# The end of an attention and feed-forward kernel: block transposes on VectorE, halves in the last tile, and another rule table

## The chip, the cores and the metric

The kernel runs on one core of one Trainium2 chip. The time is the device time of one execution in microseconds. Five engines work side by side: TensorE (PE, matmuls and the weight loads that go with them), VectorE (DVE), ScalarE (ACT), GpSimd (POOL) and SyncE (SP, which issues nearly all DMAs). Each engine runs its own instructions in the order in which they were written down; semaphores order the engines against each other.

## The reference

One transformer block with modulated layernorms, on 2048 tokens of width 512, in bfloat16. What matters of it:

```python
mod = (_silu(c) @ w_mod).reshape(c.shape[0], 6, 1, -1)       # sa, ca, ga, sb, cb, gb
h = _layernorm(x) * (1 + ca) + sa
qkv = h @ wqkv                                               # 32 heads of 16
p = softmax(q @ k.T * 16 ** -0.5);  o = p @ v                # all 2048 keys for every query
x = x + ga * (o @ wo)
h = _layernorm(x) * (1 + cb) + sb
x = x + gb * ((gelu(h @ w_gate) * (h @ w_up)) @ w_down)      # inner width 1792
```

The costly part is the softmax: 32 x 2048 x 2048 exponentials, cut below into 2048 blocks of 128 x 512.

## The kernel before, in words

**Units, rounds, blocks.** The queries are cut into seven sets (`SETS`): two of 512, three of 256, two of 128 queries. A unit is one set and one "quad" of four heads (`qd`, 0 to 7); the four heads lie on four groups of 32 partitions. For `qd` 0 and 1 the last two sets form one unit. A unit walks over the keys in rounds of four blocks, a block being 128 x 512 scores. The whole stream has 2048 blocks, and `pos` is the number of the next one.

A block goes through three steps. PE makes the scores (`qk`, into one of six banks of `ps_sc`). Then the exponential: either ACT takes two or three blocks in one instruction (`E<-ps_sc`), or DVE takes a block by a bit trick (`bits`, a TENSOR_SCALAR from `ps_sc` to uint16) and finishes four of them together with two masks and a product on 128 x 2048 (`power_task`). Last, PE multiplies with the values and with a column of ones (`pv_mms`), so that the accumulator `ps_pv` holds for each head 16 output rows and one row, number `DH` = 16, with the softmax's denominator.

**Who sets the order.** The program is planned while it is built. `stream` keeps a predicted time for each engine (`model`) and picks PE's next work step by step: scores for ACT, scores for DVE, attention matmuls, or side work (projections, output projection, feed-forward of finished sets, in windows that `plan` sets). `task` holds DVE, ACT and SP steps that wait for their operands; `urgency` orders them. The choices are governed by `RULES`, one row for every 64 positions, 32 rows in all, with the fields

```python
_Rule = collections.namedtuple("_Rule", "ready hole back fill lag early alone ahead side2")
```

`fill` is the column floor: `short(t)` is `fill` minus the columns that PE has streamed in the last 3413 ns of predicted time (a matmul on a quarter of the array counts a quarter). When it is above zero and ACT has enough work ahead, PE gets a filler matmul whose result nobody reads (`ps_mi<-xs,ident` and the like). `early` and `alone` bound when a block is given to DVE (beside ACT's blocks, or alone), `back` and `ahead` how many quads of blocks DVE may have open and how far ahead, `lag` when side work goes first.

**The end of a unit.** `unit_end` copies the accumulator to `osb`. For most units the denominators then go to DRAM and back (`scr_den`, `den`), are inverted as 128 x m numbers, go out again and come back spread over the 16 rows of each head (`rb`), and DVE multiplies. The last units have no time for that: for `PEN` (quads 6 and 7 of set 5, quads 5, 6 and 7 of set 6) `near_end` spreads the denominator with an fp32 matmul with a selection matrix (`self32`) on PE, DVE takes the reciprocal of the whole 128 x 128 result and multiplies into `onorm`. `near_end` runs as side work in the window of set 5, between the pieces of `side_last`, and for the very last quad first of all in `tail_end`.

**The tail.** After the last attention matmul two generators share PE: `tail_end` for set 6 (the last tile of 128 tokens) and `tail_rest` for what is left of the feed-forward of set 5. `tail_end` makes the output projection of its tile in one bank (a residual matmul, then one product per quad), the layernorm (`ln_stat`, `ln2_steps`, the norm into `E`), two pairs of transposes on PE, each pair into one bank, four modulations (ACT and DVE in turn), and `tail_ffn`: gate matmuls, gelu on ACT, up matmuls, product on DVE, down projection of 512 columns in one bank, `down_fin` (times `gb`, plus the residual, one DMA out). `tail_rest` has gate and up results of set 5 stored (`gate5`, `up5`); in four pieces it takes the gelu (`g5`), the product (`p5`) and the down projection. Products 0 and 1 wait for the last quad's `onorm`, products 2 and 3 for the last norm (`ln2`); the next product is posted when the piece before has been issued.

The recorder (`rec`) makes two engines that read the same bank of PSUM wait for each other.

## Time and profile before

| | us |
|---|---|
| median of 3 runs (lowest, highest) | 821.74 (820.31, 822.78) |
| the profiled execution, its own time | 824.7 |
| its span, first to last instruction | 823.0 |
| ACT busy | 793.5 (96%) |
| DVE busy | 756.9 (92%) |
| PE busy (pipelined, so not at its peak) | 752.0 (91%) |
| first exponential, last exponential's end | 16.4, 801.13 |
| mean granted TensorE clock | 0.99 |

The span is the stretch between the first and the last instruction of the profiled execution; all times of the trace count from its start. A row of the timeline has start, length, engine, line of the kernel, operation, and output <- inputs with their shapes; a bracket behind it is the idle time ahead and what ended it. A row by form has instead the number of instructions, their busy time in us and the mean of one in ns. Lines 375, 394, 398, 406 and 415 are helpers (`mm`, `act`, `tt`, `ts`, `copy`) through which most instructions go, so rows are told apart by the names of their tiles.

### The profile page before, as it was taken

The numbers are of one execution on the slowest core, as the hardware profiler recorded it, in microseconds if no ns is written. First come the engines' busy times: TensorE is split into PE (matmuls) and PEld (weight loads), VectorE is DVE, ScalarE is ACT, GpSimd is POOL, SyncE is SP. The second block draws the span as 40 slices with busy tenths as digits, with TensorE's granted clock in tenths as the row PEclk, the third lists the DMA queues.
The fourth block names the chain that finished last, engine by engine and source line by source line (L and its number), as shares of the span: only waits on it lengthen the run. The fifth ranks groups of instructions, "written<-read, shape, count | busy, mean of one in ns | idle before, by whom it ended". The sixth has DMA issues, their size and how long they took to land.

```text
span 823.0 us, 30418 instructions
## 1 busy us (share of the span) xinstructions
PE 752.0 (91%) x13786; PEld 302.8 (37%) x13788; DVE 756.9 (92%) x1366; ACT 793.5 (96%) x743; POOL 4.6 (1%) x13
## 2 busy tenths in 40 slices
PE   8899999988898998899988989999999898999997
PEld 3333333322222222222233333333543354356574
DVE  7757999999999999999999999999999999799775
ACT  5989999999999999999999999999999999999992
POOL 2000000000000000000000000000000000000000
PEclk9979999999999999999999999999999999999999
DMA  8101000000001311110003212110653242330000
GB/s 283 51 2 29 16 11 9 3 10 9 9 10 35 107 49 35 41 47 21 17 17 97 62 48 57 45 35 12 175 162 98 69 128 87 85 101 11 18 10 14
DMA packets 77212, 43.73 MB, mean 53 GB/s; under 512 B 21269, under 2 KB 75482, under 8 KB 77082
## 3 DMA queue, kind: packets, MB, share of 16 engines
q1 hardware_dynamic: 77080, 41.78, 18.0%
q8 instruction: 108, 1.77, 0.9%
q14 instruction: 22, 0.18, 0.1%
q10 hardware_dynamic: 2, 0.00, 0.0%
HBM read 39.15 MB, written 2.60 MB: 51 GB/s over the span
## 4 chain that ended last, share of the span: by engine, by line
ACT 75%; PE 19%; DVE 5%; issue 0%; DMA 0%; DVEq 0%
ACT E L394 73%; PE ps_sc L375 9%; PE ps_mi L375 7%; PE ps_pv L375 3%; ACT hreg L394 2%; DVE mreg L406 1%; ACT L394 1%; DVE dreg L406 1%; PE ps_mi L379 0%; DMA xs<-in_A_x_dram 0%; DVE st L434 0%; DVE hreg L415 0%; DVE mreg L398 0%; DVE wo L422 0%; DVE wreg L398 0%
## 5 line engine op out<-in xcount | busy, mean ns | idle before, releaser
L394 ACT ACTIVATE E<-ps_sc 128x1024 bf16<-128x1024 f32 (+1 forms) x702 | 747.2, 1291 | 8.8 <-PE ps_sc L375 8.3
L375 PE MATMUL ps_sc<-qT,kmo 32*128 32x256 bf16 (+2 forms) x1728 | 199.8, 295 | 27.2 <-ACT E L394 23.6
L375 PE MATMUL ps_sc<-qT,kme 32*128 32x256 bf16 (+2 forms) x1728 | 193.1, 295 | 22.0 <-ACT E L394 18.6
L406 DVE TENSOR_SCALAR mreg<-ps_sc 128x512 uint16<-128x512 f32 x256 | 171.4, 685 | 12.6 <-PE ps_sc L375 10.5
L375 PE MATMUL ps_pv<-E,vaug 128*17 128x256 bf16 (+2 forms) x2720 | 148.6, 291 | 0.9 <-DVE osb L415 0.6
L375 PE MATMUL ps_mi<-wreg,mreg 128*32 128x256 bf16 (+2 forms) x1872 | 107.5, 327 | 2.6 <-DVE hreg L415 1.2
L375 PEld LDWEIGHTS ps_sc<-qT,kme 32*128 32x128 bf16 x1728 | 56.5, 92 | 144.5 <-ACT E L394 123.5
L406 DVE TENSOR_SCALAR dreg<-ps_sc 128x512 uint16<-128x512 f32 x156 | 104.0, 684 | 4.8 <-PE ps_sc L375 3.3
L375 PEld LDWEIGHTS ps_sc<-qT,kmo 32*128 32x128 bf16 x1728 | 58.3, 92 | 132.8 <-ACT E L394 112.4
L375 PEld LDWEIGHTS ps_pv<-E,vaug 128*17 128x17 bf16 x2720 | 53.6, 89 | 55.1 <-issue 40.1
L406 DVE TENSOR_SCALAR mreg<-mreg 128x2048 uint16<-128x2048 uint16 x100 | 67.8, 683 | 0.2
L375 PEld LDWEIGHTS ps_mi<-wreg,mreg 128*32 128x32 bf16 (+1 forms) x1872 | 41.9, 96 | 42.3 <-issue 18.8
L375 PE MATMUL ps_pv<-mreg,vaug 128*17 128x256 bf16 (+2 forms) x856 | 50.7, 298 | 2.4 <-DVE mreg L398 1.7
L398 DVE TENSOR_TENSOR mreg<-mreg 128x2048 bf16<-128x2048 bf16 x36 | 43.6, 1216 | 0.1
L398 DVE TENSOR_TENSOR mreg<-dreg,mreg 128x2048 bf16<-128x2048 bf16 x34 | 41.1, 1209 | 0.0
L375 PE MATMUL ps_mi<-hreg,wreg 128*32 128x512 bf16 x480 | 40.3, 393 | 0.8 <-DVE qT L406 0.5
L415 DVE CAST hreg<-ps_mi 128x512 bf16<-128x512 f32 x49 | 33.6, 686 | 2.1 <-PE ps_mi L375 1.6
L398 DVE TENSOR_TENSOR dreg<-mreg,dreg 128x2048 bf16<-128x2048 bf16 x27 | 32.7, 1213 | 0.0
L375 PE MATMUL ps_mi<-wo,onorm 128*32 128x512 bf16 x416 | 31.0, 383 | 1.1 <-DVE wreg L398 0.5
L398 DVE TENSOR_TENSOR hreg<-ps_mi,hreg 128x512 bf16<-128x512 f32 x46 | 31.5, 685 | 0.3 <-PE ps_mi L375 0.2
L406 DVE TENSOR_SCALAR dreg<-dreg 128x2048 uint16<-128x2048 uint16 x44 | 29.9, 680 | 0.0
L375 PE MATMUL ps_mi<-mreg,hreg 128*32 128x512 bf16 x352 | 28.8, 384 | 0.0
(174 smaller groups left out, 689.7 us busy)
## 6 DMA issues: line engine op xcount, KB each, us to landing
mreg<-in_B_w_up_dram SPq DMA_DIRECT2D x32, 256.0 KB, 2.9
mreg<-in_B_w_gate_dram SPq DMA_DIRECT2D x28, 256.0 KB, 3.5
mreg<-in_B_w_down_dram SPq DMA_DIRECT2D x16, 256.0 KB, 2.7
dreg<-in_B_w_down_dram SPq DMA_DIRECT2D x12, 256.0 KB, 4.8
mreg<-in_w_mod_dram SPq DMA_DIRECT2D x1, 2048.0 KB, 12.0
rb<-scr_rec SPq DMA_DIRECT2D x64, 32.0 KB, 1.8
out_dram<-xs SPq DMA_DIRECT2D x16, 128.0 KB, 1.8
rb<-scr_rec SPq DMA_DIRECT2D x104, 16.0 KB, 1.7
```

The lines of the kernel that those rows point to most:

```text
L375: return self.rec("pe", lambda e: e.matmul(out, lhsT, rhs, start=start, stop=stop, tile_position=tp), [lhsT, rhs, *after], [out], cost=(n, ...
L394: return self.rec("act", lambda e: e.activation(out, in_, func, scale=scale, **kw), rd, wr, cost=self.cost("act", out, [in_], "act") + load)
L398: return self.rec(eng, lambda e: e.tensor_tensor(out, a, b, op), [a, b], [out], cost=self.cost(eng, out, [a, b], "tt"))
L406: return self.rec(eng, lambda e: e.tensor_scalar(out, a, s1, s2, **kw), rd, [out], cost=self.cost(eng, out, [a], "ts") + (60 if len(rd) > ...
L415: return self.rec(eng, lambda e: e.tensor_copy(out, in_), [in_], [out], cost=self.cost(eng, out, [in_], "ts"))
```

## The change

1. **Normalisation of the `PEN` quads.** `near_end` and its places in the side work are gone. `unit_end` transposes the accumulator in blocks of 32 x 32 on DVE, from PSUM into `osb`; a query is then a partition, and its denominator one column. DVE inverts 128 x 4 numbers, multiplies with them broadcast, into bf16, and transposes the blocks back into `onorm`. The three later steps are one task of the urgent class.
2. **The last tile.** The norm is written as two halves of 256 columns. Each of the four transposes has a bank of its own (5, 3, 2, 1). The down projection accumulates two halves of 256 columns in two banks (`ps_mi` and bank 2), and each half has its own product, addition and DMA, 64 KB each.
3. **Products of set 5.** Products 0 to 2 wait for the last `onorm`, product 3 for the norm; all four are posted ahead of the down projection.
4. **The rule table.** 23 of the 32 rows have other values. Row 0's floor goes from 2700 to 4200, row 28's from 2000 to 3900; three others (rows 12, 18 and 20) go down to 3600; the lowest floor in the table is 3300.
5. `TAILPV`, `TIE` and `GRP` are new names that have, at the values given, the effect of what stood there before.

```diff
-    (30, 50, 8, 2700, 1536, 400, 3200, 20, 1800),
-    (80, 100, 8, 4200, 1536, 400, 3200, 20, 2500),
+    (80, 300, 8, 4200, 1536, 400, 1600, 20, 1800),
+    (80, 50, 8, 4200, 1536, 400, 1600, 20, 3200),
...
-    (60, 200, 8, 3900, 2048, 500, 1900, 20, 2500),
-    (60, 50, 8, 3300, 768, 500, 1900, 12, 2500),
-    (80, 200, 8, 3300, 1536, 850, 3200, 12, 3200),
-    (30, 300, 8, 3300, 1536, 850, 1900, 28, 3200),
-    (30, 300, 8, 3300, 1536, 850, 1900, 28, 3200),
-    (30, 200, 8, 3300, 768, 850, 3200, 16, 3200),
-    (15, 200, 8, 3900, 2048, 500, 1900, 24, 2500),
-    (30, 200, 9, 3600, 2048, 500, 2500, 24, 2500),
-    (30, 200, 8, 4200, 2048, 500, 3200, 24, 2500),
-    (30, 200, 8, 4200, 1536, 500, 3200, 24, 2500),
+    (30, 200, 8, 3600, 2048, 500, 1300, 20, 1800),
+    (60, 50, 8, 3300, 768, 500, 1900, 12, 3200),
+    (80, 200, 8, 3300, 1536, 850, 3200, 12, 1024),
+    (30, 300, 8, 3300, 1536, 850, 4000, 28, 3200),
+    (30, 300, 8, 3300, 1536, 850, 4000, 28, 3200),
+    (5, 200, 8, 3300, 768, 850, 1600, 16, 3200),
+    (15, 200, 8, 3600, 2048, 500, 1900, 24, 2500),
+    (30, 200, 9, 3600, 2048, 500, 2500, 24, 1800),
+    (15, 200, 8, 3600, 2048, 500, 1600, 24, 3200),
+    (30, 200, 8, 4200, 1536, 500, 4000, 24, 2500),
...
-    (80, 200, 10, 3600, 2048, 650, 2500, 24, 1800),
+    (5, 50, 7, 4200, 2560, 850, 1900, 20, 700),
...
-    (80, 300, 8, 2000, 1536, 500, 2500, 16, 2500),
-    (80, 100, 10, 3900, 1536, 300, 2500, 32, 2500),
-    (45, 200, 8, 3300, 1024, 300, 2500, 24, 1024),
-    (80, 100, 10, 3900, 1536, 300, 2500, 32, 1800),
+    (80, 300, 6, 3900, 3500, 500, 2500, 16, 2500),
+    (80, 50, 10, 4200, 2048, 650, 1900, 20, 1800),
+    (80, 50, 10, 4200, 3500, 0, 1900, 20, 1800),
+    (80, 50, 11, 4200, 3500, 1100, 1900, 20, 1800),
...
+    def blocks32(self, out, in_):
+        return self.rec("dve", lambda e: e.transpose(out, in_), [in_], [out], cost=self.cost("dve", out, [in_], "bn"))
...
+        if src is not None:
+            dst = self.normed(k, 0)
+            return steps + [lambda h=h: self.ln_norm(a, dst[:, h], src[:, h]) for h in (slice(0, 256), slice(256, D))]
...
+    def down_half(self, bank, t, h, i, x):
+        if x == 0:
+            self.tt("dve", self.xw[:, h], bank, self.gb[:, h], ALU.mult)
+            return
+        self.tt("dve", self.xs[:, t, h], self.xs[:, t, h], self.xw[:, h], ALU.add)
+        self.dma("sp", self.out[0, P * t:P * t + P, h], self.xs[:, t, h], "out%d" % ((t + i) % 4))
...
+        if len(sets) == 1 and qd in PEN.get(sets[0], ()):
+            self.blocks32(osb, acc[:, 0:W])
+            k = sets[0]
+            part = osb.rearrange("p (b r) -> p b r", r=32)
+            norm = rb.bitcast(BF16)[:, 0:W]
+            rec = self.rden[:, b, o:o + m]
+
+            def back():
+                self.blocks32(self.onorm[:, qd, OCOL[k]:OCOL[k] + W], norm)
+                if self.probing is None:
+                    self.live.pop(u)
+            self.task([lambda: self.recip(rec, part[:, :, DH]),
+                       lambda: self.tt("dve", norm.rearrange("p (b r) -> p b r", r=32), part,
+                                       rec.rearrange("p (b o) -> p b o", o=1).broadcast_to([P, m, 32]), ALU.mult),
+                       back], ("onorm", k, qd))
+            return
...
+PART5 = (0, 4, 8, 12, NFC)
+WHEN5 = (("onorm",), ("onorm",), ("onorm",), ("ln2",))
...
-        early, late = self.after([("onorm", last, 7)]), self.after([("ln2", last)])
-        when = (early, early, late, late)
+        when = [self.after([WHEN5[j] + (last, 7)[:1 + (WHEN5[j] == ("onorm",))], ("g5", j)]) for j in range(len(part))]
...
-        for h in range(2):
-            pb = self.scp[:, 4 + h, :]
-            yield lambda h=h, pb=pb: self.transp(pb, lambda t: self.normed(k, t), 1, h)
-            for i in range(2):
-                dc = 2 * h + i
-                self.modulate("act" if i == 0 else "dve", self.t2T[:, dc, c0:c0 + W],
-                              pb.bitcast(BF16)[:, W * i:W * i + W], self.modB, dc)
-        yield from self.tail_ffn(k, self.mi[:, :], (0, 1, 2, 3, 4, 5), 4)
+        for dc in range(NDC):
+            pt = self.scp[:, (5, 3, 2, 1)[dc], :].bitcast(BF16)[:, 0:W]
+            yield lambda dc=dc, pt=pt: self.transpose(pt, self.normed(k, 0)[:, P * dc:P * dc + P], self.ident[:, :])
+            self.modulate("act" if dc % 2 == 0 else "dve", self.t2T[:, dc, c0:c0 + W], pt, self.modB, dc)
+        yield from self.tail_ffn(k, (self.mi[:, 0:256], self.scp[:, 2, 0:256]), (0, 1, 2, 3, 4, 5), 4)
```

## The prediction

> **What bounds the kernel now.** I read the chain of waits first, then cut the span at the first exponential (16.4 us), at the two ends of the one stretch where ScalarE (ACT) is visibly idle, and at the last exponential (801.13 us).

> ```profile
> ACT 75%; PE 19%; DVE 5%; issue 0%; DMA 0%; DVEq 0%
> ...
> 16.40:37.90 21.50, 16.71 (x239) 5.88 (x239) 17.89 (x58) 21.50 (x20) 0.00 (x0) 1.00 0.33 123
> 37.90:52.60 14.70, 14.37 (x151) 5.56 (x150) 7.49 (x19) 10.38 (x10) 0.00 (x0) 0.54 0.00 1
> 52.60:801.13 748.53, 690.76 (x13051) 273.63 (x13054) 708.44 (x1224) 746.92 (x689) 0.31 (x1) 1.00 0.18 49
> 801.13:823.00 21.87, 16.36 (x217) 10.76 (x203) 11.62 (x28) 6.73 (x13) 0.00 (x0) 1.00 0.04 14
> ```

> In the windows the engines stand in the order PE, weight loads, VectorE (DVE), ACT, POOL, then the granted clock. From 52.60 to 801.13 ACT is idle for 748.53 - 746.92 = 1.6 us: nothing but less ACT work, that is exponentials moved to DVE, can shorten that stage. Two places are different. Between 37.90 and 52.60 ACT stands still for 14.70 - 10.38 = 4.32 us while the granted clock is 0.54. After 801.13 comes a tail of 21.87 us in which no engine is full and a serial chain decides.

> **The clock drop.** The half clock holds for 51.58 - 37.93 = 13.65 us, four times 3.41 us, so I laid windows of 3.41 us on its edges.

> ```profile
> 31.10:34.52 3.42, 2.51 (x30) 0.67 (x28) 3.25 (x12) 3.42 (x4) 0.00 (x0) 1.00 0.02 5
> 34.52:37.93 3.41, 2.26 (x24) 0.64 (x25) 3.30 (x17) 3.41 (x4) 0.00 (x0) 1.00 0.00 0
> 37.93:41.34 3.41, 3.41 (x25) 1.61 (x24) 2.48 (x9) 3.14 (x3) 0.00 (x0) 0.50 0.00 0
> ...
> 51.58:55.00 3.42, 3.19 (x38) 1.21 (x39) 2.72 (x6) 2.93 (x4) 0.00 (x0) 1.00 0.01 2
> ```

> The window just ahead of the drop has TensorE (PE) at 2.26 of 3.41 us. Its matmuls by form, and the exponentials that ACT had done since 16.4 us:

> ```profile
> L375 PE MATMUL ps_pv<-E,vaug 128*17 128x512 bf16 x8 | 0.8, 385 | 0.0
> L375 PE MATMUL ps_sc<-qT,kmo 32*128 32x512 bf16 x5 | 0.8, 384 | 1.2 <-ACT E L394 1.2
> L379 PE MATMUL ps_mi<-ident,dreg 128*128 128x128 bf16 x4 | 0.6, 238 | 0.0
> L375 PE MATMUL ps_sc<-qT,kme 32*128 32x512 bf16 x3 | 0.4, 385 | 0.1
> L375 PE MATMUL ps_mi<-xs,ident 128*32 128x512 bf16 x4 | 0.4, 379 | 0.0
> ...
> L394 ACT ACTIVATE E<-ps_sc 128x1536 bf16<-128x1536 f32 x10 | 15.8, 1578 | 0.0
> L394 ACT ACTIVATE E<-ps_sc 128x1024 bf16<-128x1024 f32 x10 | 11.4, 1138 | 0.0
> ```

> A matmul on 32 rows or 17 or 32 columns fills a quarter of the array, so the planner counts a quarter of its columns: (8 + 5 + 3 + 4) x 512 / 4 + 4 x 128 = 3072 columns. The planner's own log works in the same 3413 ns (`short`), and the rule in force sets how many columns it keeps in them. ACT had done 10 x 3 + 10 x 2 = 50 blocks of 512 columns, so the position is below 64 and row 0 of the table rules: its floor is 2700, the second lowest of the 32. 3072 satisfies it, and no filler is due. The change sets 4200 there. Going from 3072 to 4200 takes 1128 / 512 = 2.2 more fillers (the x4 row is one: four quarter matmuls at once, 0.4 us), 0.9 us, and PE has 3.41 - 2.26 = 1.15 us idle in the window. The filler goes out only while the planner sees slack on ACT, so I cost it at nothing; without that cover it would be at most the 0.9 us a window.

> [...]

> The gain is bounded by 0 (the drop stays) and 4.32 us (all ACT idle there). Part of the idle time is k projections that the next key group needs; DVE, at 3.30 of 3.41 us with their layernorm, paces those at any clock. I take **3.9 us**.

> **The tail.** What follows the last attention matmul, from the timeline, and one row by form:

> ```profile
> 802.03 0.29 DVE L415 COPY osb<-ps_pv 128x128 f32<-128x128 f32 x1 [0.28 <-PE ps_pv L375]
> ...
> 802.38 0.49 PE L375 MATMUL ps_sc<-osb,self 128*128 128x128 f32 x2 [0.40 <-DVE osb L415]
> ...
> 802.90 0.96 DVE L418 RECIPROCAL rb<-ps_sc 128x128 f32<-128x128 f32 x1 [0.38 <-PE ps_sc L375]
> 802.92 1.46 PE L375 MATMUL ps_sc<-wo,onorm 128*128 128x512 bf16 x6
> 803.89 0.29 DVE L398 TENSOR_TENSOR onorm<-osb,rb 128x128 bf16<-128x128 f32 x1
> 804.10 0.42 DVE L398 TENSOR_TENSOR hreg<-hreg 128x512 bf16<-128x512 bf16 x1
> ...
> 804.43 0.38 PE L375 MATMUL ps_sc<-wo,onorm 128*128 128x512 bf16 x1
> ...
> 804.85 0.70 DVE L434 BATCH_NORM_STATS2 st<-ps_sc 128x6 f32<-128x512 f32 x1 [0.32 <-PE ps_sc L375]
> ...
> 805.68 0.39 DVE L398 TENSOR_TENSOR hreg<-hreg 128x512 bf16<-128x512 bf16 x1
> ...
> 807.26 0.81 DVE L406 TENSOR_SCALAR E<-ps_sc,mv,rstd 128x512 bf16<-128x512 f32 x1
> ...
> 808.12 0.40 PE L379 MATMUL ps_sc<-ident,E 128*128 128x128 bf16 x4 [0.96 <-DVE E L406]
> 808.45 0.81 ACT L394 ACTIVATE wreg<-ps_sc,modB 128x128 bf16<-128x128 bf16 x2 [2.21 <-PE ps_sc L379]
> ...
> 809.01 0.69 DVE L406 TENSOR_SCALAR wreg<-ps_sc,modB 128x128 bf16<-128x128 bf16 x2 [0.61 <-ACT wreg L394]
> ...
> L418 DVE RECIPROCAL rden<-den 128x4 f32<-128x4 f32 x3 | 0.5, 167 | 0.0
> ```

> *Normalisation.* Before: copy, fp32 sum on PE, a reciprocal of 128x128, a product; 802.03 to 803.89 + 0.29 = 804.18, 2.15 us. After, on DVE alone: block transpose, reciprocal of 128x4 (0.17), product (0.29), block transpose back, with some 0.03 between dependent steps. No row shows a DVE transpose. From below the copy of the same 128x128 shape, 0.29; from above the slowest row on that shape, the reciprocal, 0.96. It moves data as the copy does, so I take 0.29: 0.29 + 0.17 + 0.29 + 0.29 + 0.1 = 1.14, done at 803.17. With 0.96 each it would be 2.48, done at 804.51.

> [...]

> *The wait that follows.* PE's output projection no longer stands behind the sum. The residual matmul and seven of the eight products start right behind the attention matmuls, about 801.85 (an estimate: their result reaches the copy at 802.03 some 0.2 us after issue) instead of 802.92, at 0.216 apart (six span 1.46, the last lasting 0.38: 1.08 / 5). Eight of them hold PE until 803.58, later than 803.17: PE is now what is late, and the last product goes out at 803.6 instead of 804.43. The statistics start 0.83 us earlier. (With transposes of 0.96 they would start 0.1 us later than now.) The steps from statistics to norm (2.41 us) are the same; one product of the other tile stands in them (805.68, 0.39) and still may, as its later wait is only dropped for the third piece.

> *Norm in halves.* 512 columns take 0.81. At 1.07 ns a column, from the copy (128 columns, 0.29) to the statistics (512, 0.70), a half takes about 0.54, and the next instruction starts some 0.08 before one ends (the product at 803.89 lasts 0.29, the one behind it starts at 804.10). Counted from the norm's start: first half done 0.54, second 1.0 (0.81 before, later). The transposes, each in a bank of its own, give ACT its first piece at 0.92, 0.27 earlier than the 808.45 - 807.26 = 1.19 of now. More counts that DVE no longer waits for ACT's reading of a shared bank (the 0.61 of idle before 809.01). ACT 0.92 and 1.38, DVE 0.99 and 1.44, all done at 1.83; now 809.01 + 0.69 - 807.26 = 2.44. That is 0.61 us. Bounds: 0 if the extra instruction eats it, 0.8 if DVE is quite free.

> *Down projection in halves.*

> ```profile
> 818.94 0.59 PE L375 MATMUL ps_mi<-hreg 128*128 128x512 bf16 x2
> 819.58 0.69 DVE L398 TENSOR_TENSOR wreg<-ps_mi,gb 128x512 bf16<-128x512 f32 x1 [0.87 <-PE ps_mi L375]
> 820.30 0.42 DVE L398 TENSOR_TENSOR xs<-xs,wreg 128x512 bf16<-128x512 bf16 x1
> 820.75 0.36 SPq L444 DMA_DIRECT2D out_dram<-xs  x1
> ```

> 28 matmuls of 256 columns stream what 14 of 512 did. The first half's product (about 0.42) runs while the second half finishes, but four DVE instructions replace two, and SP issues two DMAs, 0.36 us each, the second behind the first. I take 0.1 us, bounds -0.3 and +0.4. Tail: 0.83 + 0.61 + 0.1 = **1.5 us**, between 0.3 and 2.0.

> **The middle.** Five quads lose 0.29 + 0.96 + 0.29 of DVE for 0.29 + 0.17 + 0.29 + 0.29: 5 x 0.50 = 2.5 us of DVE freed, and five sums of PE (0.49 each). What DVE time buys:

> ```profile
> L406 DVE TENSOR_SCALAR mreg<-ps_sc 128x512 uint16<-128x512 f32 x256 | 171.4, 685 | 12.6 <-PE ps_sc L375 10.5
> L406 DVE TENSOR_SCALAR dreg<-ps_sc 128x512 uint16<-128x512 f32 x156 | 104.0, 684 | 4.8 <-PE ps_sc L375 3.3
> L406 DVE TENSOR_SCALAR mreg<-mreg 128x2048 uint16<-128x2048 uint16 x100 | 67.8, 683 | 0.2
> L398 DVE TENSOR_TENSOR mreg<-mreg 128x2048 bf16<-128x2048 bf16 x36 | 43.6, 1216 | 0.1
> ...
> L394 ACT ACTIVATE E<-ps_sc 128x1024 bf16<-128x1024 f32 x441 | 431.6, 1156 | 1.5 <-PE ps_sc L375 1.4
> L394 ACT ACTIVATE E<-ps_sc 128x1536 bf16<-128x1536 f32 x227 | 329.3, 1568 | 0.4 <-PE ps_sc L375 0.2
> ```

> A quad (four blocks) on DVE takes 4 x 0.685 + 2 x 0.683 + 1.216 = 5.3 us and frees 4 x (1.568 - 1.156) = 1.65 us of ACT. 2.5 us buy 0.47 quads, **0.8 us**. The other rules decide how many quads there are: 412 blocks, 103 quads now. DVE's idle 748.53 - 708.44 = 40 us would hold 7.5 more (12 us); a table that gives DVE fewer costs 1.65 each without a floor in the trace. Rows go both ways (the `alone` bound, above which DVE takes blocks by itself, falls in nine rows and rises in rows 15, 16 and 21), so I take 0 and allow two quads, 3.3 us, either way.

> **Sum.** 3.9 + 1.5 + 0.8 = 6.2 us. The profiled execution took 824.7 us; it would take 818.5. It stands 3.0 above the median of 821.74, so against the median I forecast **815.5 us**.

> **Rivals.**
> 1. The clock drop stays. For it: the floor is kept in the planner's predicted time, and PE has room only where ACT's lead lets fillers out. Against: with floors of mostly 3300 and more the middle ran at a mean of 1.00 (the 52.60 row). Price 3.9: 819.4.
> 2. Slower: the table gives DVE fewer quads. Place: ACT from 52.60 to 801.13, full already, so each lost quad is 1.65 us on the end. For it: `early` falls from 300 to 0 in row 30, `alone` doubles in rows 15 and 16. Against: the end has idle DVE and row 31 goes the other way. It decides from 824.2 on, 8.7 / 1.65 = 5.3 quads, fewer than 391 blocks on DVE; with six lost, 825.4.
> 3. The DVE transpose is near the upper bound: tail 0.4 instead of 1.5, 816.6.
> 4. The table fills idle DVE: three quads more, 810.5.

> **How the numbers follow.** Forecast 0.55 (its own range 812.2 to 818.8, the two quads either way), rival 1 0.17, rival 2 0.06, rival 3 0.10, rival 4 0.12. What a measurement here can tell from no change is 0.3%, 2.5 us, so faster means below 819.3. Rival 1 sits on that edge: a third of it counts as faster, with the forecast and rivals 3 and 4: 0.82; same 0.12; slower 0.06. The range goes to 811.0 (into rival 4) and 820.6 (over rival 1).

> **What would show it.** Granted clock 1.00 from 37 to 52 us, ACT idle below 1 us there, more filler rows on `xs,ident` in it. Last exponential 4 to 5 us earlier. In the tail: two DVE transposes near 0.29, the statistics about 2.0 us after the last attention matmul instead of 2.9, PE the releaser; the last modulation 1.8 us after the norm's start. Wrong if the half clock stands before 60 us, or if the DVE block count leaves 404 to 420.

## The result, and the profile after

The changed kernel takes 817.76 us (median of 9 runs, 815.88 to 819.57); the kernel before, run beside it, 822.78 us (9 runs, 820.31 to 826.14). The ratio is 0.9935, with a 95% interval of 0.9918 to 0.9953: faster by 5.0 us, between 3.9 and 6.7. A second measurement, taken with the last runs below, gave 0.9940 (0.9921 to 0.9959). The profiled execution after took 816.2 us, its span is 814.5 us.

The windows of the changed kernel, cut as those of before were: at the first exponential, at both ends of the stretch where the clock was low, and at the end of the last exponential.

```profile
16.20:37.90 21.70, 19.79 (x294) 7.05 (x291) 17.93 (x60) 21.70 (x20) 0.00 (x0) 1.00 0.33 122
37.90:52.60 14.70, 13.48 (x211) 5.31 (x209) 10.28 (x21) 14.19 (x14) 0.00 (x0) 1.00 0.01 3
52.60:794.84 742.24, 685.33 (x13029) 270.70 (x13022) 702.96 (x1223) 741.91 (x685) 0.31 (x1) 1.00 0.18 49
794.84:814.50 19.66, 15.88 (x197) 11.40 (x183) 10.75 (x32) 6.83 (x12) 0.00 (x0) 0.98 0.05 15
```

The second row has the clock at 1.00 instead of 0.54 and ACT idle for 14.70 - 14.19 = 0.51 us instead of 4.32. In the third ACT is idle for 742.24 - 741.91 = 0.33 us instead of 1.6. The tail is 19.66 us instead of 21.87.

The fillers of 512 columns between 16 and 52.6 us by form, first of the kernel before, then of the changed one (those on `nil` have zeros for weights and are added to a running sum, which they leave as it is):

```profile
L375 PE MATMUL ps_sc<-xs,ident 128*32 128x512 bf16 x16 | 1.8, 502 | 0.2 <-ACT E L394 0.2
L375 PE MATMUL ps_mi<-xs,ident 128*32 128x512 bf16 x20 | 1.8, 383 | 0.0
```

```profile
L380 PE MATMUL ps_sc<-xs,ident 128*32 128x512 bf16 x36 | 2.9, 384 | 0.4 <-ACT E L399 0.4
L380 PE MATMUL ps_pv<-xs,nil 128*17 128x512 bf16 x32 | 2.8, 382 | 0.0
L380 PE MATMUL ps_mi<-xs,ident 128*32 128x512 bf16 x32 | 2.5, 383 | 0.0
```

36 quarter matmuls have become 100: the higher floor does what it says. The two sets of DVE's exponentials, over the whole of the changed kernel:

```profile
L411 DVE TENSOR_SCALAR mreg<-ps_sc 128x512 uint16<-128x512 f32 x252 | 167.9, 683 | 11.4 <-PE ps_sc L380 9.5
L411 DVE TENSOR_SCALAR dreg<-ps_sc 128x512 uint16<-128x512 f32 x160 | 106.9, 684 | 9.5 <-PE ps_sc L380 8.5
```

252 + 160 = 412 blocks, as many as before (256 + 156).

Where the 824.7 - 816.2 = 8.5 us between the two profiled executions lie is read from the time at which the n-th exponential block ends, counted in both traces:

```
block            53      80     1152    1280    1920    2048
before        38.93   55.36   447.86  500.30  743.67  801.13
after         38.45   50.54   443.04  495.09  740.58  794.83
difference    -0.48   -4.82    -4.82   -5.21   -3.09   -6.31
```

0.48 us is the start, which varies from execution to execution: in a second profile of the changed kernel (819.24 us) block 53 ends 0.10 later than before. Blocks 53 to 80, the stretch of the low clock, give 4.34. Nothing happens from there to block 1152. 0.39 more comes at 488 us, where the profile before had a second, shorter drop (488.49 to 491.90). From block 1280 to the last the difference grows by 1.10, not evenly: 2.1 us are lost by block 1920 and regained behind it. The second profile of the changed kernel has only 0.31 of this 1.10. The tail gives 2.21, and in the second profile it is as long as here (19.67 us).

The tail in the timeline of the changed kernel (start, length, engine, line, operation, output <- inputs):

```profile
795.21 0.39 PE L380 MATMUL ps_sc<-xs,ident 128*128 128x512 bf16 x1
...
795.32 0.32 DVE L427 STREAM_TRANSPOSE osb<-ps_pv 128x128 f32<-128x128 f32 x1
795.43 1.89 PE L380 MATMUL ps_sc<-wo,onorm 128*128 128x512 bf16 x8
795.67 0.18 DVE L423 RECIPROCAL rden<-osb 128x4 f32<-128x4 f32 x1
795.88 0.29 DVE L403 TENSOR_TENSOR rb<-osb,rden 128x128 bf16<-128x128 f32 x1
...
796.21 0.31 DVE L427 STREAM_TRANSPOSE onorm<-rb 128x128 bf16<-128x128 bf16 x1
...
797.36 0.70 DVE L442 BATCH_NORM_STATS2 st<-ps_sc 128x6 f32<-128x512 f32 x1
...
798.19 0.39 DVE L403 TENSOR_TENSOR hreg<-hreg 128x512 bf16<-128x512 bf16 x1
...
798.57 0.42 DVE L403 TENSOR_TENSOR hreg<-hreg 128x512 bf16<-128x512 bf16 x1
...
799.98 1.00 DVE L411 TENSOR_SCALAR E<-ps_sc,mv,rstd 128x256 bf16<-128x256 f32 x2
...
801.09 0.61 DVE L411 TENSOR_SCALAR wreg<-ps_sc,modB 128x128 bf16<-128x128 bf16 x2
...
801.23 0.60 PE L380 MATMUL ps_pv<-hreg 128*128 128x512 bf16 x2
```

The normalisation runs from 795.32 to 796.52, 1.20 us, in four DVE steps; the eight products of PE end at 797.32, 0.8 later, and the statistics follow at 797.36. The norm's halves start at 799.98 and the last modulation ends at 801.09 + 0.61 = 801.70.

### The profile page after: what moved, and what is told of

It reads as the page before. It is cut to its first block, busy times and chain, and to the rows that moved or that the text cites. A ratio compares the mean times of both kernels' runs of the same rounds, so it can differ in the third digit from the quotient of the medians.

```text
span 814.5 us, 30576 instructions
## 1 busy us (share of the span) xinstructions
PE 747.7 (92%) x13864; PEld 301.4 (37%) x13864; DVE 753.7 (93%) x1374; ACT 792.9 (97%) x743; POOL 4.6 (1%) x13
## 4 chain that ended last, share of the span: by engine, by line
ACT 83%; PE 11%; DVE 5%; DMA 1%; issue 0%; SPq 0%; DVEq 0%
ACT E L399 79%; PE ps_sc L380 5%; PE ps_mi L380 4%; ACT hreg L399 2%; DVE mreg L411 2%; PE ps_pv L380 2%; ACT L399 1%; DVE dreg L411 1%; DMA mreg<-in_w_mod_dram 1%; DVE mreg L403 1%; DVE hreg L403 0%; DVE hreg L420 0%; DVE wo L430 0%; DVE wreg L411 0%; DVE hreg L411 0%
## 5 line engine op out<-in xcount | busy, mean ns | idle before, releaser
L380 PE MATMUL ps_sc<-qT,kmo 32*128 32x256 bf16 (+2 forms) x1728 | 197.5, 293 | 24.9 <-ACT E L399 21.2
L380 PE MATMUL ps_sc<-qT,kme 32*128 32x256 bf16 (+2 forms) x1728 | 194.4, 293 | 19.8 <-ACT E L399 16.2
L411 DVE TENSOR_SCALAR mreg<-ps_sc 128x512 uint16<-128x512 f32 x252 | 167.9, 683 | 11.4 <-PE ps_sc L380 9.5
L411 DVE TENSOR_SCALAR dreg<-ps_sc 128x512 uint16<-128x512 f32 x160 | 106.9, 684 | 9.5 <-PE ps_sc L380 8.5
L411 DVE TENSOR_SCALAR mreg<-mreg 128x2048 uint16<-128x2048 uint16 x100 | 67.8, 681 | 0.2
L420 DVE CAST hreg<-ps_mi 128x512 bf16<-128x512 f32 (+1 forms) x49 | 33.0, 673 | 2.3 <-PE ps_mi L380 1.8
L380 PE MATMUL ps_mi<-wo,onorm 128*32 128x512 bf16 x448 | 34.2, 384 | 0.5 <-DVE onorm L403 0.5
## 6 DMA issues: line engine op xcount, KB each, us to landing
mreg<-in_w_mod_dram SPq DMA_DIRECT2D x1, 2048.0 KB, 12.1
```

The lines of the kernel that those rows point to most:

```text
L380: return self.rec("pe", lambda e: e.matmul(out, lhsT, rhs, start=start, stop=stop, tile_position=tp), [lhsT, rhs, *after], [out], cost=(n, ...
L411: return self.rec(eng, lambda e: e.tensor_scalar(out, a, s1, s2, **kw), rd, [out], cost=self.cost(eng, out, [a], "ts") + (60 if len(rd) > ...
L420: return self.rec(eng, lambda e: e.tensor_copy(out, in_), [in_], [out], cost=self.cost(eng, out, [in_], "ts"))
```

## The experiments

The kernel before ran beside each group of runs: 823.34 us for the first four runs, 822.79 for the next four, 822.20 for the last four (35, 35 and 13 executions). Ratios are against it, with 95% intervals. The mean granted clock of one execution is given where the clock is in question.

**The table alone, and the code alone.** The kernel before with the whole new table, and the changed kernel with the whole old one:

```diff
 RULES = (
-    (30, 50, 8, 2700, 1536, 400, 3200, 20, 1800),
+    (80, 300, 8, 4200, 1536, 400, 1600, 20, 1800),
...                       (all 32 rows; the second run does the reverse)
```

> The kernel before with the whole new rule table and nothing else. If the floor of row 0 keeps the clock up (my theory), the half clock before 60 us is gone and the exponentials from block 53 to block 80 take 12.1 us instead of 16.4 us as in the profile of the changed kernel: about 4.3 us less than before, with the tail unchanged (last exponential to end 21.9 us); in medians of runs, in which other clock drops come and go, 3 to 4.5 us less. Rival (the gain is in the tail or in blocks moved to VectorE): within 1 us of the kernel before, or a block count on VectorE that is not 412.

> The changed kernel with the old rule table. Theory: the half clock from about 38 to 51 us is back, all that is gained is the tail, 1.5 us by the forecast and 2.2 us by the profile of the changed kernel (21.87 to 19.66 us from the last exponential to the end): 1.5 to 2.5 us below the kernel before. Rival (the table is worth nothing): the same as the changed kernel, 5 us below.

Table alone: 822.97 us, 1.0004 (0.9982 to 1.0027). Code alone: 821.90 us, 0.9985 (0.9967 to 1.0003). Neither interval excludes no change, and neither is worth what it is worth in the pair. The profile of the table alone has the clock at 1.00 throughout and its last exponential at 796.12, 5.0 us earlier than before; what it gains there it gives back behind it, as its timeline shows:

```profile
796.63 0.49 PE L375 MATMUL ps_mi<-osb,self 128*128 128x128 f32 x2
...
796.95 1.06 PE L375 MATMUL ps_sc<-wreg,mreg 128*128 128x128 bf16 x16
...
797.16 0.95 DVE L418 RECIPROCAL rb<-ps_mi 128x128 f32<-128x128 f32 x1
...
798.17 1.07 PE L375 MATMUL ps_mi<-wreg,mreg 128*128 128x128 bf16 x16
...
798.85 0.95 DVE L418 RECIPROCAL rb<-ps_sc 128x128 f32<-128x128 f32 x1
...
802.56 0.70 DVE L434 BATCH_NORM_STATS2 st<-ps_sc 128x6 f32<-128x512 f32 x1 [0.75 <-PE ps_sc L375]
```

Two sums on PE, two reciprocals of 0.95 and the up projections of set 5 (the `wreg,mreg` rows) stand behind the last exponential, the statistics start 6.4 us after it (3.7 in the kernel before), and the tail is 820.7 - 796.12 = 24.6 us. The code alone, with all the old rows, has the short tail (817.6 - 797.83 = 19.8) and the unsteady clock of before: a mean of 0.992 over its runs, as the kernel before had.

**The floor of the first row.** The changed kernel with that one number put back:

```diff
-    (80, 300, 8, 4200, 1536, 400, 1600, 20, 1800),
+    (80, 300, 8, 2700, 1536, 400, 1600, 20, 1800),
```

> The changed kernel with one number put back: row 0's column floor 2700 instead of 4200. Theory: a window of 3.41 us below about 3100 columns comes back between 29 and 38 us, the half clock with it, and 3 to 4.3 us of the gain are lost, so that it is 1 to 2 us below the kernel before. Rival (other fields or rows of the table do it): as fast as the changed kernel, 5 us below the kernel before.

819.18 us, 0.9966 (0.9943 to 0.9989); the clock of single executions goes from 0.983 to 1.000, with a mean of 0.995. Its profiled execution, like that of the code alone, lost one window early and none at 38 us. The window of the code alone, then that of this kernel:

```profile
19.03:22.45 3.42, 3.31 (x27) 0.60 (x25) 2.67 (x13) 2.84 (x3) 0.00 (x0) 0.50 1.02 407
```

```profile
19.02:22.43 3.41, 3.41 (x29) 0.56 (x29) 2.51 (x11) 2.66 (x3) 0.00 (x0) 0.50 1.02 408
```

With the low floor the drop is not fixed at 38 us: whether and where it comes changes from one execution to the next. The 13.65 us in the profile before were one case.

**Columns or busy time.** The changed kernel with its order and all its instructions kept, only that a filler sent before block 64 streams 16 columns instead of 512 (its result is read by nobody):

```diff
+        if self.thin:
+            return self.rec("pe", lambda e: e.matmul(out[:, 0:16], lhsT, rhs[:, 0:16], ...), ...)
```

> The changed kernel with its order of instructions as it is on every engine; only the filler matmuls issued before block 64 stream 16 columns instead of 512 (their results are read by nobody). Theory (columns streamed set the clock): half clock before 60 us, 3 to 5 us slower than the changed kernel, so 0 to 2 us below the kernel before. Rival 1 (the new order itself is better and the fillers are idle weight): as fast as the changed kernel, 5 us below. [...]

823.29 us, 1.0006 (0.9986 to 1.0026); all 12 executions have a mean clock of 0.988 or less. Its windows:

```profile
17.51:20.93 3.42, 1.86 (x34) 0.66 (x32) 3.11 (x13) 3.42 (x4) 0.00 (x0) 1.00 1.03 405
20.93:27.75 6.82, 6.82 (x61) 2.82 (x62) 2.82 (x7) 6.07 (x6) 0.00 (x0) 0.50 0.21 80
27.75:31.17 3.42, 3.42 (x88) 1.53 (x84) 2.71 (x5) 3.19 (x4) 0.00 (x0) 1.00 0.00 0
31.17:34.58 3.41, 2.31 (x56) 0.85 (x44) 3.26 (x11) 3.41 (x4) 0.00 (x0) 1.00 0.02 5
34.58:51.65 17.07, 16.49 (x191) 5.94 (x183) 10.73 (x37) 13.20 (x12) 0.00 (x0) 0.50 0.00 1
```

Half clock twice, each time behind a window in which PE was busy for 1.86 or 2.31 us. In the first of them PE is idle for 3.42 - 1.86 = 1.56 us in all. Without the streamed columns the gain is gone (a ratio of 1.0006 instead of 0.9935), so it is the fillers' columns that hold the clock in this kernel.

The reverse, in the kernel before: its order kept, each filler before block 64 sent three times over.

```diff
+        if self.thick:
+            return self.rec("pe", lambda e: [e.matmul(out, lhsT, rhs, ...) for _ in range(3)][-1], ...)
```

> The kernel before in its own order; each filler matmul issued before block 64 is sent three times in a row (9 groups of fillers become 27). Theory (columns streamed set the clock): clock 0.997 or more against 0.9926 over the runs of the kernel before, 1.5 to 3 us faster than before. Rival 1 (the new order of the changed kernel makes the clock's difference, not the columns): clock and time as before. Rival 2 (the extra matmuls stand in ACT's way): clock up, time the same or longer.

823.46 us, 1.0003 (0.9985 to 1.0021), with a mean clock of 0.9965 instead of 0.993. The drop at 38 us is gone from the profile (a short one, 18.50 to 21.91, is there), but ACT pays for the columns in another coin, in the window up to 37.9 us:

```profile
16.40:37.90 21.50, 18.46 (x269) 6.85 (x269) 15.85 (x46) 19.39 (x18) 0.00 (x0) 0.92 0.36 131
```

ACT is idle there for 21.50 - 19.39 = 2.11 us, where it was full before: block 53 ends at 41.63, 2.70 later, and of the clock's gain 0.93 is left at the last block. Not all of this is the fillers' doing: the short drop has its part. The code alone and the changed kernel with the low floor have a drop at the same place without the extra columns, and counted from the end of the first block they are 1.01 and 1.03 us later than before at block 53, this kernel 2.48. Some 1.5 us are left for the columns. That a filler costs nothing where the planner has counted it is seen in the changed kernel, where ACT is full in this window.

**Front and end of the table.** The kernel before with rows 0 to 22 new, and the changed kernel with rows 23 to 31 old:

```diff
 RULES = (
-    (30, 50, 8, 2700, 1536, 400, 3200, 20, 1800),
+    (80, 300, 8, 4200, 1536, 400, 1600, 20, 1800),
...                       (rows 0 to 22 in the kernel before)

-    (30, 50, 8, 4200, 768, 500, 3200, 20, 2500),
+    (30, 50, 8, 4200, 1536, 500, 3200, 20, 2500),
...                       (rows 23 to 31 in the changed kernel)
```

> The kernel before with rows 0 to 22 of the new rule table; the last nine rows and all code as before. Theory after the first four runs (the front rows hold the clock, the last rows are made for the new normalisation, and with the old one they leave side work behind the last exponential): mean granted clock 0.998, the last exponential and the tail as in the kernel before, so all of the clock's worth, 2 to 3 us below the kernel before in medians. Rival (the clock is worth nothing in the end, as the whole table alone suggested with 822.97): the same as before.

> The changed kernel with the last nine rows of the rule table (from block 1472 on) as before. Theory: clock as in the changed kernel, tail as in the changed kernel (19.7 us from the last exponential), and only what the last rows bring is lost, 1 to 1.5 us: 3.5 to 4.5 us below the kernel before. Rival (the last rows bring nothing by themselves, they only fail with the old normalisation): 5 to 5.5 us below, as the changed kernel.

New front in the kernel before: 820.96 us, 0.9973 (0.9956 to 0.9990), mean clock 0.999. This is the front of the table by itself, and it holds the clock. In its profile the difference to the profile before is -4.51 us at block 80, -4.94 at block 1920 and -4.98 at the last, but over the runs 1.8 us are left. Its tail is 818.5 - 796.16 = 22.3 us, 0.5 longer than before: DVE's first step of it, the copy, comes at 797.55, 1.39 us after the last exponential instead of 0.90.

Old end in the changed kernel: 823.46 us, 1.0008 (0.9990 to 1.0025), the whole gain gone although the clock mostly holds (0.997). By block counts its lead over the profile before falls from 5.27 to 2.42 us between blocks 1920 and 1984, and its tail is 823.29 - 798.84 = 24.45 us. The timeline of that tail:

```profile
799.01 3.02 SPq L452 DMA_DIRECT2D rb<-scr_rec  x4
...
799.55 0.32 DVE L427 STREAM_TRANSPOSE osb<-ps_pv 128x128 f32<-128x128 f32 x1 [1.77 <-PE ps_pv L380]
...
803.31 0.29 DVE L403 TENSOR_TENSOR onorm<-osb,rb 128x128 bf16<-128x128 f32 x1 [1.03 <-DMA rb<-scr_rec]
...
803.90 1.03 PE L380 MATMUL ps_sc<-wo,onorm 128*128 128x512 bf16 x4
804.96 0.70 DVE L442 BATCH_NORM_STATS2 st<-ps_sc 128x6 f32<-128x512 f32 x1 [1.36 <-PE ps_sc L380]
```

Here a quad whose denominators go through DRAM is finished so late that its factors come back only at 803.3; four products and the statistics wait for them, and the new normalisation, done at 800.44 + 0.31 = 800.75, gains nothing. The statistics start 804.96 - 798.84 = 6.1 us after the last exponential, in the changed kernel 2.5; another 1.2 us goes behind them (18.33 us to the end instead of 17.14), where PE ran at half clock from 808.80 to 812.21, behind 3.41 us in which it had been busy for only 0.84. The old last rows are not enough for this: with all the old rows the same code has a tail of 19.8 us. They fail behind the new front rows; why a plan that starts otherwise ends so, no run shows.

**More columns in the middle.** In the profile of the changed kernel the fewest columns in 3.41 us, over any placement of such a stretch, lie near 95 and 481 us (2336 and 2304, of matmuls that start in it). The planner is told of three fillers in place of one in a step there:

```diff
-        self.mm(mi[:, P:D], self.ident[:, :], self.xs[:, NT - 1, P:D])
+        for _ in range(3):
+            self.mm(mi[:, P:D], self.ident[:, :], self.xs[:, NT - 1, P:D])
```

> The changed kernel with three fillers of 384 columns instead of one behind each of the four groups of one-column matmuls that make the second modulation (94 to 98 us). In the changed kernel's trace the sum of columns over 3.41 us falls to 2336 there, below 3072 for 0.29 of all placements of such a window, and to 2304 at 480 us for 0.35 of them; nowhere else for more than 0.03. Theory: the first of the two places is mended, so runs with a clock drop become about half as many and the median falls by 0.3 to 1 us below the changed kernel's 817.76. Rival (TensorE has no room there and ACT waits): ACT idle at 94 to 98 us, same or slower than the changed kernel.

826.01 us, 1.0040 (1.0022 to 1.0058): slower, with a clock of 0.997 or more in every execution. The planner shifted all that follows: 264 + 144 = 408 blocks on DVE, and a tail as long as that of the table alone:

```profile
52.60:799.59 746.99, 689.66 (x13046) 268.52 (x13043) 697.97 (x1206) 744.62 (x686) 0.31 (x1) 1.00 0.18 49
799.59:823.90 24.31, 20.30 (x310) 16.30 (x304) 14.85 (x41) 6.94 (x12) 0.00 (x0) 1.00 0.05 14
```

The same columns without the planner knowing of them (its order kept), and zero-weight matmuls ahead of the attention matmuls of blocks 1240 to 1271, beside the changed kernel run again:

```diff
...                       (the fillers at 94 to 98 us three times, as above)
+        if self.pad and not start:
+            z = self.nil[:, 0:VW]
+            return self.rec("pe", lambda e: [e.matmul(out, x, rhs, ...) for x in (z, lhsT)][-1], ...)
...
+            self.pad = 1240 <= pos < 1272
```

> The changed kernel with its planned order kept on every engine (the planner is not told), and more columns at the two places where its sums over 3.41 us fall below 3072: each filler behind the second modulation's one-column matmuls (94 to 98 us) three times, and before each accumulating attention matmul of blocks 1240 to 1272 (around 480 us) one with zero weights. Theory (what is left of the clock's loss sits there): granted clock 0.9995 or more in nearly all runs, 0.3 to 1.2 us below the changed kernel. Rival (the extra matmuls stand in ACT's way, or the order slips): ACT idle there, no faster than the changed kernel.

> The changed kernel itself, beside the next one on the same chip: 5 us below the kernel before, mean granted clock near 0.999, a clock drop in about half of the runs.

Changed kernel again: 817.44 us, 0.9940 (0.9921 to 0.9959). More columns: 819.07 us, 0.9960 (0.9946 to 0.9975), with the clock at 1.00 in all 8 executions, and still 1.6 us slower than the kernel it was to improve. Its window around the first place:

```profile
90.00:100.00 10.00, 9.51 (x151) 3.83 (x151) 9.17 (x16) 9.62 (x10) 0.00 (x0) 1.00 0.06 15
```

ACT is idle there for 0.38 us, and for 0.20 between 475 and 481; in the changed kernel it is busy for all of the 10 and the 6 us. The loss by block counts is 1.1 us between blocks 128 and 256. The wait that runs over the end of this window makes up most of the rest: from 90 to 101 us ACT is idle for 11.00 - 10.11 = 0.89 us. In the profile of the changed kernel run again the clock did fall at both places:

```profile
95.62:99.03 3.41, 3.41 (x60) 1.76 (x57) 3.31 (x5) 3.41 (x4) 0.00 (x0) 1.00 0.00 0
99.03:102.45 3.42, 3.42 (x33) 0.77 (x30) 2.27 (x8) 3.15 (x3) 0.00 (x0) 0.50 0.00 0
...
484.74:488.15 3.41, 3.41 (x38) 1.08 (x34) 2.15 (x4) 3.41 (x2) 0.00 (x0) 0.50 0.05 4
```

By the block counts of the two profiles these drops cost 0.89 and 0.76 us.

**The two halves.** The changed kernel with the last norm whole, its transposes again in two pairs of one bank each, and with the last down projection whole:

```diff
-            return steps + [lambda h=h: self.ln_norm(a, dst[:, h], src[:, h]) for h in (slice(0, 256), slice(256, D))]
+            return steps + [lambda: self.ln_norm(a, dst, src)]
...                       (and the transposes in pairs)

-        yield from self.tail_ffn(k, (self.mi[:, 0:256], self.scp[:, 2, 0:256]), (0, 1, 2, 3, 4, 5), 4)
+        yield from self.tail_ffn(k, self.mi[:, :], (0, 1, 2, 3, 4, 5), 4)
...                       (and one product, one addition and one DMA for it)
```

> The changed kernel with the last norm in one piece and its transposes in two pairs of one bank each, as before. By the prediction's step the last modulation ends 2.44 us after the norm's start instead of 1.83 (1.72 in the changed kernel's trace), and the stretch from the last exponential to the end is 0.6 to 0.7 us longer than 19.65 us. Rival (TensorE has other work in that time): less than 0.2 us.

> The changed kernel with the last down projection in one piece of 512 columns, one bank, one product, one addition, one DMA of 128 KB. By the prediction's step the stretch from the last exponential to the end is 0.1 us longer than 19.65 us; bounds 0.3 us shorter (the second DMA behind the first is saved) to 0.4 us longer.

One run each. Whole norm: 819.52 us, a tail of 817.80 - 797.52 = 20.28, 0.62 longer. Whole down projection: 817.47 us, a tail of 815.75 - 795.92 = 19.83, 0.17 longer. Of the whole norm's timeline:

```profile
802.67 0.81 DVE L411 TENSOR_SCALAR E<-ps_sc,mv,rstd 128x512 bf16<-128x512 f32 x1
...
804.42 0.69 DVE L411 TENSOR_SCALAR wreg<-ps_sc,modB 128x128 bf16<-128x128 bf16 x2 [0.75 <-PE ps_pv L380]
```

From the norm's start to the end of the last modulation it is 804.42 + 0.69 - 802.67 = 2.44 us, what it was in the kernel before; in halves it is 1.72. The norm in halves, with its four banks, is worth what the tail showed. For the down projection 0.17 us in one run is little against the scatter of the tail: 19.66 to 19.75 us in the profiles that share it.

## Why the prediction was right, and where it was off

The time came out 2.3 us above the forecast of 815.5 and inside its range; the sign and two of the three places, the clock and the tail, were right. That the total came so near is in part luck: the clock was taken 1.5 us too high and the tail 0.7 too low, and the middle's 0.8 does not come from where it was looked for. The forecast also started from a median of three runs, 821.74; over nine runs the kernel before takes 822.78, and of the 6.2 us forecast 5.0 came.

**The clock: right in place and sign, mis-sized in the sum.** The term was 3.9 us and the profiles show 4.34 for the stretch, with the signs that were named: clock 1.00, ACT idle 0.51 us, 100 fillers for 36. The failing step is the last one, "it stands 3.0 above the median of 821.74, so against the median I forecast 815.5": it takes off the median what a single execution lost. The 35 executions of the kernel before beside the first four runs show what the drop is worth over runs. Their mean clock lies between 0.983 and 1.000; a line through them is 820.0 us plus 4.2 us per 0.01 of clock missing. Their mean of 0.9926 against 0.9987 in the changed kernel's 9 runs makes 0.61 x 4.2 = 2.6 us. The front of the table alone brought 1.8, with 0.5 given back in its tail: 2.3. So the term is about 2.4, not 3.9 (an estimate from these two). That the profiled execution stood 3.0 us above the median was the sign that it had lost more than most, and it was noted and not used. The last exponential, forecast 4 to 5 us earlier, comes 6.3 us earlier in the first profile of the changed kernel and 3.3 in the second.

Fillers as the cause of the clock are shown from both sides: with 16 columns the gain is gone, with row 0's floor put back the clock is unsteady again, and with more columns in the old order its mean rises from 0.993 to 0.9965. That they were costed at nothing held in the planner's order, and only there: sent three times over without the planner, they cost ACT some 1.5 us. The 3072 columns that the prediction counts in the window ahead of the drop take in whole matmuls that lie partly outside it; by the share inside the window they are 2905, and this matters for the bound at the end of this text. Rival 1, in which the drop stays, is out for 38 us; at 95 and 481 us the changed kernel still has drops in some executions.

**The tail: 2.2 us instead of 1.5.** Its steps against those predicted:

| step | forecast | measured |
|---|---|---|
| last exponential to DVE's first step (0.90 to 0.49) | not forecast | +0.41 |
| first step to statistics (2.82 to 2.04) | 0.83 | 0.78 |
| statistics to norm (2.41 to 2.62) | 0 | -0.21 |
| norm to last modulation (2.44 to 1.72) | 0.61 | 0.72 |
| last modulation to the end (13.30 to 12.78) | 0.1 | 0.52 |

The DVE transpose is 0.32 us from fp32 in PSUM and 0.31 in bfloat16, near the lower bound that was taken; rival 3 is out. The chain took 1.20 us for a forecast 1.14, and PE's eight products were late next, as said. Two products of set 5, at 798.19 and 798.57, now lie between statistics and norm, not one. The last line was under-sized: halves are worth 0.17 of it at most, by the one run with the whole down projection. Most of the rest fits the last two down products of set 5, which now run at 801.23, ahead of the gates, and stood at 809.99 in the profile before. The prediction read the new waits of set 5's parts only for what they did to the norm. No run undid that alone.

**The middle: no quad was gained.** The term was 0.8 us, from 0.47 more quads on DVE. DVE has 412 blocks as before, so the step from freed DVE time to more blocks on DVE failed. What the profile of the changed kernel gains behind block 1280, 1.1 us, is ACT's idle time there: 1.30 us before (300.83 - 299.53), 0.19 after. It is not steady: in the second profile of the changed kernel ACT is idle there for 1.02 us and 0.31 is gained. Rivals 2 and 4, fewer or more quads, are out. Where rival 2 looked, ACT's middle, no blocks were lost, but the last rows, whose `early` and `alone` it doubted, do harm in another way, told next.

**The parts don't add, which the sum assumed.** Table alone brings nothing that can be told from zero (ratio 1.0004), code alone about 1.4 us (823.34 - 821.90, ratio 0.9985, up to 1.0003), together 5.0. Where the new table meets the old normalisation, sums and up projections come late; where the changed code meets the new front and the old last rows, a quad through DRAM does. Both tails are some 24.5 us. With all the old rows the changed code has the short tail, and so it is neither the old nor the new last rows that make a long one, but last rows behind a plan for which they were not made. The middle's sum (a 0.5 us saving per quad, turned into ACT time) had no term for that.

Adding the measured terms, 2.4 for the clock, 2.2 for the tail and 0.3 to 1.1 behind block 1280, gives 4.9 to 5.7; the runs show 5.0, between 3.9 and 6.7.

None of the versions tried is shown to be faster than the changed kernel; the whole down projection, with 817.47 us in one run, cannot be told from it. Two held the clock better and lost more than that by ACT's waiting or by another plan.

## What to carry to other kernels

A stall or a gain that is seen in one profile is worth its mean over executions, not its size in that one: compare the granted clock of many runs, and where the profiled run stands off the median, ask which of its stalls is the odd one. A table of ordering rules that fits one plan is a part of that plan; price it with the code it was made for, and look behind the last exponential for what a good middle has pushed there. Work added to hold a clock is free only on an engine that nobody waits for at that moment: the fillers that the planner had counted left ACT full up to 37.9 us (21.70 of 21.70), those sent three times over cost some 1.5 us.

## What the runs showed of the hardware

**In these profiles the clock goes by columns, not by busy time.** In the window ahead of the drop at 99.03 in the changed kernel run again, PE is busy for 3.41 of 3.41 us (the row 95.62 above), and the clock still falls. Its matmuls by form:

```profile
L380 PE MATMUL ps_sc<-qT,kmo 32*128 32x512 bf16 x9 | 1.6, 384 | 0.0
L380 PE MATMUL ps_mi<-sc_bf,mreg 128*128 128x1 bf16 x32 | 1.4, 165 | 0.0
L380 PE MATMUL ps_mi<-xs,ident 128*32 128x384 bf16 x16 | 1.4, 336 | 0.0
L380 PE MATMUL ps_sc<-qT,kme 32*128 32x512 bf16 x3 | 0.8, 384 | 0.1
```

32 matmuls of one column fill 1.4 us and stream 32 columns. With a quarter for the matmuls on a quarter of the array the whole matmuls add up to 12 x 128 + 16 x 96 + 32 = 3104; counted by the share of each that lies inside the window they are 2856. PE's busy time does not tell such windows apart. The first row is of the kernel before, where the clock fell behind the window, the second of the changed kernel with the old end, where it stayed:

```profile
485.08:488.49 3.41, 1.85 (x44) 0.68 (x36) 3.41 (x8) 3.38 (x3) 0.00 (x0) 1.00 0.28 78
481.12:484.53 3.41, 1.86 (x34) 0.78 (x34) 3.41 (x8) 3.38 (x3) 0.00 (x0) 1.00 0.30 83
```

By shares the first has 2727 columns, the second 3653. The fewest with which a window kept the clock are those at 32.69 in the code alone (PE busy 2.37 us):

```profile
L380 PE MATMUL ps_sc<-qT,kme 32*128 32x512 bf16 x8 | 1.2, 384 | 0.7 <-ACT E L399 0.6
L380 PE MATMUL ps_pv<-E,vaug 128*17 128x512 bf16 x8 | 0.8, 385 | 0.0
L380 PE MATMUL ps_sc<-xs,ident 128*32 128x512 bf16 x4 | 0.4, 390 | 0.2 <-ACT E L399 0.2
L380 PE MATMUL ps_mi<-xs,ident 128*32 128x512 bf16 x4 | 0.4, 379 | 0.0
```

**The steps of the grid don't start with the kernel.** With the low floor the clock fell at 19 us, at 38 or, with a mean of 1.000 over the run, hardly at all; over 35 executions of the kernel before the mean went from 0.983 to 1.000. The drops last whole steps: 3.42 us the one at 19.03, 13.65 = 4 x 3.41 the one at 38. Counted in steps of 3.4133 us (436.91 / 128) from the first instruction, the edges lie behind a step by 0.38 us in the profile before (37.93 = 11 x 3.4133 + 0.38), by 1.96 in that of the code alone (19.03), by 1.43 with each filler sent three times (18.50). The two profiles of the changed kernel, one program in one order, have 1.23 (the clock falls at 813.60, behind PE's last matmul) and 0.04 (99.03). So the grid cut the same program at another place in these two executions. What follows for a forecast, that a window with few columns is a chance and not a fixed price, is what the prediction left out.
